# Q rows: two masked copies out of PSUM on VectorE, or one copy and two masks on GpSimd

## The chip, the cores and the metric

The kernel runs on one core of a Trainium2 chip. The metric is the device time of one execution, in microseconds (us); the time of a kernel is the median of several runs. A core has a matrix engine (PE, TensorE), which writes to PSUM; a vector engine (DVE, VectorE); an activation engine (ACT, ScalarE); GpSimd (POOL); and queues that start DMA transfers, most of them here on SyncE (SP). Each engine works through its own list of instructions in order and waits at semaphores for the others.

## The reference

Two identical transformer layers over one sequence of 2048 rows of 512 values, with 32 heads of 16 and a feed-forward width of 1792, all inputs in bf16:

```python
def _A_ref(x, wqkv, wo):                     # B, S, D = 1, 2048, 512; H = 32; Dh = 16
    qkv = (x @ wqkv).reshape(B, S, 3, H, Dh).transpose(2, 0, 3, 1, 4)
    q, k, v = qkv[0], qkv[1], qkv[2]
    scores = jnp.einsum("bhqd,bhkd->bhqk", q, k) * (Dh ** -0.5)
    p = _softmax(scores, axis=-1)
    o = jnp.einsum("bhqk,bhkd->bhqd", p, v)
    return o.transpose(0, 2, 1, 3).reshape(B, S, D) @ wo

def _B_ref(x, w_gate, w_up, w_down):         # F = 1792, gelu by tanh
    return (_gelu(x @ w_gate) * (x @ w_up)) @ w_down

x = x + _A_ref(_layernorm(x), A_wqkv, A_wo)
x = x + _B_ref(_layernorm(x), B_w_gate, B_w_up, B_w_down)
# ... and both once more, with the same weights
```

## The kernel before

**Units and tiles.** Attention is cut into units: one block of 512 queries (four per layer) and one group of four heads (eight per block), so 32 units per layer. A unit has 64 score tiles of 128 keys x 512 queries, 16 key tiles for each of its four heads. In the last block of the second layer a tile holds two key tiles of 256 queries instead, so that this block ends in two halves. Keys lie on the rows of a tile, queries on its columns.

**Scores and Q.** A head has only 16 rows of Q and K. PE is used in four row groups of 32, and each holds two heads, so one chunk of 128 rows holds eight heads: those of two units. To score one of the two heads of a row group, the rows of the other one must be zero in Q. So Q of a chunk is kept twice: copy 0 holds rows 0 to 15 of each 32 and zeros below, copy 1 the other way round. The function `qproj` builds the piece of work that projects Q: four matrix products into one PSUM bank (`mm_piece`, line 664), then two VectorE instructions (line 712) that read the bank and write the two copies as f16 into two of the six slots of `Q`. Each multiplies by a column of `QMASK`, [128, 2], which holds the scale `QSCALE` on the rows to keep and zero on the others. `QSCALE` carries the softmax scale and log2(e) x 1024, so that a score is a power of two in units of 1/1024. When both copies are there, `kept` announces the Q; the first twelve units' copies of the second layer are stored to DRAM (line 288, SP's queue) and read back later.

**Exp, on two engines.** Score products (line 1565) fill slots of three or two PSUM banks in turn, which ACT turns into exps with one instruction (line 1579, into `PT`). A further tile can go to a vector bank: DVE adds a bias, clips at zero and writes int16 (line 1619, into `PI`). Read as f16, these bits are a piecewise linear power of two. For its error three more copies are made, with the exponent shifted by one, two and three quarters of an octave (line 1659, into `PP`, SBUF to SBUF, up to four tiles in one instruction). All four are multiplied into V, the shifted ones into copies of V that are scaled down accordingly (`VD`, made by GpSimd, line 754). So a tile on ACT takes one product with V (called PV, line 1711), and a tile on DVE four. PV products of the four heads stand side by side in four column groups of PE and add up in bank 7; an extra column of ones in V gives the sum of exps. The sum of a unit is copied out (lines 1006 and 1011), sent through DRAM, divided by its sums of exps on GpSimd (line 967) and multiplied by `wo`.

**Other work.** Projections of K, Q and V, output products, and the feed-forward blocks (lines 1233 and 1297, evacuated by DVE at lines 1252, 1276 and 1328) are pieces that PE fits in between. Banks 5 and 6, when free, serve these pieces and the vector tiles. When PE has nothing to do, `keep_clock` adds a product with zeros into bank 7 (line 1731).

**The planner.** The order on every engine is decided before the program is built, by a Python loop that simulates all engines with fixed costs: an instruction of DVE or GpSimd has its cost as the last entry of its job. `vector_tile` allows a vector tile only if DVE's backlog (waiting jobs, and 0.48 us for each waiting shift) is below `DVE_LATE`. `fill_ready` says when the next slot may be filled; it may wait for a vector bank as long as ACT stays `WAIT_D` ahead. `pick` chooses the tiles of a slot, `flush` closes a group of shifts. `port_at` keeps the shifts of DVE and the work of GpSimd apart in the plan. `fit` is how many PV passes go before the next fill, and `post_tol` how far a feed-forward piece may run past it. `PACE` and `behind` set how fast each block's feed-forward is worked off while the next block's attention runs. On the chip each engine keeps the planned order, whatever the true durations are.

Of the kernel before, what the change touches and what calls it, by code (L numbers as in the profile page):

```python
# [175 lines left out]
def _emit_fast(nc, es, x_in, wqkv, wo, wg, wu, wd, out, n_rep=2):  # L176
# [21 lines left out]
    VW = 17  # L198
    NPH = 4
    NPART = 12 if NQB > 1 else 0  # L200
    DVE_LATE = 2.61
    WAIT_D = 0.65
    OCT = 1024.0
    LOG2E = 1.4426950408889634
    QSCALE = OCT * LOG2E * DH ** -0.5
# [31 lines left out]
    NQS = 6  # L237
# [36 lines left out]
    def bank(b):  # L274
        return PS[:, b, :]
# [34 lines left out]
    def change(kind):  # L310
        return SW if kind_now[0] != kind else 0.0
# [68 lines left out]

    sch.op("pool", lambda e: e.memset(QMASK[:], 0.0), w=[("QMASK",)])  # L381
    for j in range(4):
        sch.op("pool", lambda e, j=j: e.memset(QMASK[32 * j:32 * j + 16, 0:1], QSCALE), r=[("QMASK",)], w=[("QMASK",)])
    sch.op("pool", lambda e: e.tensor_scalar(QMASK[:, 1:2], QMASK[:, 0:1], -1.0, QSCALE, op0=ALU.mult, op1=ALU.add),
           r=[("QMASK",)], w=[("QMASK",)])
    sch.op("dve", lambda e: e.memset(PS[:, ACC, :], 0.0), w=[BK[ACC]], cost=0.6)
    sch.op("pool", lambda e: e.memset(OKV[:], 1.0), w=[("OKV",)])
# [281 lines left out]
    def xk(b):  # L669
        return [("XNT", 4 * b + i) for i in range(4)]  # L670
# [29 lines left out]
    def qproj(layer, up):  # L700

        qb, c = min(up // NCK, NQB - 1), up % NCK
        h = up // NCK - (NQB - 1) if layer == n_rep - 1 and NQB > 1 and up // NCK >= NQB - 1 else None
        q0, qn = (0, 512) if h is None else (256 * h, 256)

        qi = up + (NPART // 2 if layer and 2 * up >= NPART else 0)

        def evac(b):
            ops = []
            for p in range(2):  # L710
                slot = (layer * NU + 2 * qi + p) % NQS
                ops.append((lambda e, p=p, slot=slot: e.tensor_scalar(Q[:, slot, q0:q0 + qn], bank(b)[:, 0:qn],  # L712
                                                                     QMASK[:, p:p + 1], None, op0=ALU.mult),
                            [BK[b], ("QMASK",)], [("Q", slot)], 0.126 + 0.001042 * qn))
            evac_job(1, b, ops, kept)

        def kept(o):
            have.add((layer, "q", qi))
            if layer and 2 * up < NPART:
                for p in range(2):  # L720
                    u = 2 * up + p
                    slot = (layer * NU + u) % NQS
                    move(2, "qs%d" % slot, QSD[u, :, :], Q[:, slot, :], [("Q", slot)], [("QS", u)], got(("qs", u)), kb=128)
        lo = 512 * qb + q0
        return mm_piece([(WQ[:, ck, 128 * c:128 * (c + 1)], XNT[:, ck, lo:lo + qn]) for ck in range(NCK)],
                        [("XNT", t) for t in range(lo // 128, (lo + qn) // 128)] + [("WQ", c)], evac, cols=qn)
# [9 lines left out]
    def vproj(layer, c, kb):  # L736
        def fn(e, bs):
            for t in range(4):
                for ck in range(NCK):
                    tt = 4 * kb + t  # L740
                    ins = e.matmul(bank(bs[0])[:, 128 * t:128 * (t + 1)], lhsT=XNT[:, ck, tt * 128:(tt + 1) * 128],  # L741
                                   rhs=WV[:, ck, 128 * c:128 * (c + 1)], start=(ck == 0), stop=(ck == NCK - 1))
            return ins

        def then(o):
            have.add((layer, "v", c, kb))
            for part, (m0, m1) in (("A", (0, NMA)), ("B", (NMA, NM))):
                if m1 == m0 or kb != (3 * m1 - 1) // 4:
                    continue
                for ph in range(1, NPH):  # L750
                    dst = VD[:, c, ph - 1, :, 4 * m0:4 * m1, :]
                    src = AP(VP, (2 * c * NKT * 4 + 12 * m0 + 2) * VW,
                             [[VP[:].ap[0][0], 128], [NKT * 4 * VW, 2], [3 * VW, 4 * (m1 - m0)], [1, VW]])
                    job("pool", 2, [(lambda e, dst=dst, src=src, ph=ph: e.tensor_scalar(  # L754
                        dst, src, 2.0 ** (-ph / NPH), None, op0=ALU.mult),
                        [("VP", c, k) for k in range(kb + 1)] + [("VPONE",)], [("VD", c, part)],
                        0.46 + 0.039 * 4 * (m1 - m0))],
                        got((layer, "vd", c, part)) if ph == NPH - 1 else None)

        def after(bs):  # L760
            b = bs[0]
            evac_job(1, b, [(lambda e: e.tensor_copy(  # L762
                VP[:, c, :, 16 * kb:16 * kb + 16, 0:16].rearrange("p r k d -> p k r d"),
                bank(b).rearrange("p (k r d) -> p k r d", r=2, d=16)),
                             [BK[b]], [("VP", c, kb)], 0.6)], then)

        return Piece(0.064 * 4 * NCK, xk(kb) + [("WV", c)], fn, after)


    PRE = 1  # L770
# [645 lines left out]
    def vector_tile():  # L1416

        if pace["haste"]:
            return False
        if not dg["items"] and pend.get(("PI", dg["n"] % NPI)):  # L1420
            return False
        late = max(0.0, sch.free["dve"] - now[0]) + sum(op[3] for j in jobs["dve"] for op in j[2])
        late += 0.48 * len(shifts)
        return late < DVE_LATE

    def vector_bank():
# [11 lines left out]
    def pick(look=False):  # L1438

        cap = slot_cap()  # L1440
        want_d = not look and started_all() and behind() < LAG and vector_tile()
        bd = vector_bank() if want_d else None
        if bd is None or sch.ready("pe", w=[BK[bd]]) > now[0] + 0.13:
            want_d = False
        a, d = [], None
        spare = None
        for k, x in enumerate(cur):
            if len(a) == cap and (d is not None or not want_d or k >= 16):
                break
            t = x[3]  # L1450
            if want_d and d is None and d_tile(x) and (not dg["items"] or dg["uk"] == x[:3]):
                if all(y[3] % 4 != t % 4 for y in a):
                    d = x
                    continue
                if len(a) == cap and spare is None:
                    spare = x
            if len(a) < cap:
                a.append(x)
            elif not want_d:
                break  # L1460
        return a, d if d is not None else spare
# [17 lines left out]
    def fill_ready():  # L1479

        s = slot_no[0] % 2
        if slot_open[s]:
            return None
        if slot_no[0] < 2 and not free_banks.issuperset(slot_banks()):
            return None
        pull()
        a, _ = pick(True)
        a = [x for x in a if k_here(x)]
        if not a:
            return None  # L1490
        if pend.get(("PT", pt_of())):
            return None
        keys = []
        for x in a:
            keys += tile_keys(x)
        ready = sch.ready("pe", keys, [BK[b] for b in slot_banks()[:len(a)]])
        if started_all() and not pace["haste"] and (free_banks or vb_busy):
            free = min([sch.ready("pe", w=[BK[b]]) for b in free_banks]
                       + [max(sch.free["dve"], now[0]) + 0.78 for b in vb_busy])
            if ready < free <= sch.free["act"] - WAIT_D:  # L1500
                ready = free
        return ready
# [43 lines left out]
    def a_slot(atiles, dtile):  # L1546
# [50 lines left out]
        if dtile is not None:  # L1597
# [13 lines left out]
            def then(o):  # L1611
# [6 lines left out]
                ripe(items, gi, done)  # L1618
            dve(0, [(lambda e: e.tensor_scalar(PI[:, gi, 512 * r:512 * (r + 1)], bank(bd), DBIAS, 0.0,  # L1619
                                               op0=ALU.add, op1=ALU.max), [BK[bd]], [("PI", gi, r)], 0.6)], then)  # L1620
        if dg["items"] and (len(dg["items"]) == 4 or seg_left[dg["uk"]] < 4 and not any(
                x[:3] == dg["uk"] and d_tile(x) for x in cur)):
            flush()

# [168 lines left out]
    def post_source():  # L1793
        while True:
            if posts:
# [3 lines left out]
                for p in posts.pop(0):  # L1799
                    if p is not None:  # L1800
                        first += 1
                        if first <= 6:
                            p.tol = 1.0
                        pace["n"] += (p.cost + 0.1) / 0.71
                    yield p
# [9 lines left out]

    A_END = NU + NPART * (NQB - 1.0) / NQB
    B_END = A_END + NPART / NQB * min(1.0, NG / max(1.0, NPART))
    LAST = 2 * NU - NG / 2 + 2.00
    STEP = (LAST - B_END - 1.0) / (NQB - 1)
    PACE = [(NU + 1.0, A_END - 1.22)]  # L1820
    for i in range(NQB - 1):
        a = max(PACE[-1][1] if i else B_END + 1.0, NU + NG * (i + 1) + 1.0 if NG * (i + 1) > NPART else B_END + 1.0)
        PACE.append((a, LAST if i == NQB - 2 else B_END + 1.0 + STEP * (i + 1)))
# [16 lines left out]
    def post_tol():  # L1840
        if pace["haste"] or behind() > LAG:
            return 99.0
        return 0.45 if behind() > 0 else 0.17

    def queue_source(queue):
        while True:
# [14 lines left out]
    while True:  # L1861
# [27 lines left out]
            limit = max(F, sch.free["act"] - 0.44) - t  # L1889
        its = pv_ready(t)  # L1890
        byj = [sum(1 for it in its if it[1] == j) for j in range(4)]
        fit = int((limit - change("col")) / MM + 0.3)
        full = min(byj)
        rest = False
        if its:
# [8 lines left out]
        keep = next((p for p in (src.peek() for src in sources) if p is not None and p.held is not None), None)  # L1904
        ready_ = keep is not None and piece_ready(keep, keep.held) <= t + 0.02 and keep.cost + change("full") <= limit + 0.1
        if not (ready_ and not press) and fit >= 1 and (full >= want or full and (rest or press)):
            pv(its, min(fit, full, 4))
            continue
        cand = None
        for src in sources:  # L1910
# [883 lines left out]
```

## Time and profile before

| | |
|---|---|
| median of 4 runs | 1593.15 us (1591.34 to 1594.07) |
| profiled execution | 1591.3 us |
| its span, first to last instruction | 1589.0 us |
| granted TensorE clock | 1.0 |
| busy: PE, DVE, ACT, POOL | 1517.0, 1431.3, 1518.5, 177.8 us |

Busy time is the time in which an engine executes an instruction of the program. A row of the groups of instructions reads: line, engine, operation, what it writes <- what it reads, shapes, count, then the busy time in us and the mean length of one in ns, then the idle time of the engine just before these instructions and what ended it. Instructions of ACT overlap their neighbours a little, so their mean times their count is more than their busy time. A line of the timeline gives the start and the length of a run of equal instructions. A line of the table by stretches gives the stretch, its length, and the busy time (and number of instructions) of PE, PEld (its weight loads), DVE, ACT and POOL.

### The profile page before, as it was taken

The page shows a single profiled execution, that of the slowest core. Times are in us where ns is not written, and L with a number is a line of the kernel's source. Part 1 is how long each engine was busy: PE and PEld are TensorE (multiplying, and loading weights), DVE is VectorE, ACT ScalarE, POOL GpSimd, SP SyncE. Part 2 cuts the span into 40 slices and gives each one's busy share as a digit, 9 for nine tenths or more (in the row PEclk, how much of TensorE's full clock was granted, in tenths as well). Part 3 has the DMA queues.
Part 4 walks back from the last instruction along what each step waited for, and adds up shares of the span by engine and source line. Part 5 has one row for each costly group of instructions (what it writes and reads, how often), then busy time and mean ns, then how long its engine had stood idle before and what let it go on. Part 6 is the DMA issues. An engine that isn't in the chain of part 4 may idle for free.

```text
span 1589.0 us, 38476 instructions
## 1 busy us (share of the span) xinstructions
PE 1517.0 (95%) x16150; PEld 504.7 (32%) x16150; DVE 1431.3 (90%) x2485; ACT 1518.5 (96%) x1308; POOL 177.8 (11%) x218
## 2 busy tenths in 40 slices
PE   8999999999999999999999999899999999999998
PEld 4332222222222222333333223222222222444455
DVE  8999999889988899988998989999889889998784
ACT  6999999999999999999999999999999999999981
POOL 2311110011100211000520001020101000100010
PEclk9999999999999999999999999999999999999999
DMA  5200111125121411122512242332332114112145
GB/s 157 61 8 5 50 35 46 55 60 114 32 61 51 124 53 28 51 55 74 119 48 67 62 107 67 98 98 78 105 83 63 48 44 129 37 48 81 51 106 170
DMA packets 168377, 112.39 MB, mean 71 GB/s; under 512 B 55048, under 2 KB 148232, under 8 KB 168200
## 3 DMA queue, kind: packets, MB, share of 16 engines
q1 hardware_dynamic: 164504, 105.28, 24.6%
q0 software_dynamic: 2112, 4.19, 1.0%
q8 instruction: 131, 2.15, 0.6%
q10 hardware_dynamic: 1584, 0.39, 0.1%
q14 instruction: 46, 0.38, 0.1%
HBM read 81.40 MB, written 19.78 MB: 64 GB/s over the span
## 4 chain that ended last, share of the span: by engine, by line
ACT 44%; PE 44%; DVE 10%; DMA 1%; issue 1%; SPq 0%; DVEq 0%
ACT fPT L1579 41%; PE fPS L1711 13%; PE fPS L1565 12%; PE fPS L1233 10%; PE fPS L1297 5%; DVE fPI L1619 4%; DVE fPP L1659 4%; PE fPS L664 2%; ACT fHT L1525 2%; PE fPS L1731 1%; PE fPS L741 1%; ACT L1525 1%; DVE fHT L1252 0%; DVE fHT L1276 0%; ACT L1579 0%
## 5 line engine op out<-in xcount | busy, mean ns | idle before, releaser
L1579 ACT ACTIVATE fPT<-fPS 128x1536 bf16<-128x1536 f32 x1265 | 1444.5, 1281 | 23.7 <-PE fPS L1565 19.7
L1619 DVE TENSOR_SCALAR fPI<-fPS 128x512 int16<-128x512 f32 x935 | 632.9, 684 | 58.8 <-PE fPS L1565 53.4
L1565 PE MATMUL fPS<-fQ,fKT 32*128 32x512 f16 (+1 forms) x4608 | 504.0, 359 | 46.2 <-ACT fPT L1579 33.6
L1659 DVE TENSOR_SCALAR fPP<-fPI 128x2048 int16<-128x2048 int16 (+3 forms) x783 | 490.8, 646 | 12.3 <-PE fPS L1711 9.0
L1711 PE MATMUL fPS<-fPT,fVP 128*17 128x512 bf16 (+1 forms) x3555 | 452.9, 358 | 4.2 <-DVE fOS L1006 1.6
L1711 PE MATMUL fPS<-fPP,fVD 128*17 128x512 f16 (+1 forms) x3159 | 441.3, 357 | 4.5 <-DVE fPP L1659 3.7
L1565 PEld LDWEIGHTS fPS<-fQ,fKT 32*128 32x128 f16 x4608 | 135.3, 91 | 524.3 <-ACT fPT L1579 394.0
L1711 PE MATMUL fPS<-fPI,fVP 128*17 128x512 f16 (+1 forms) x1053 | 267.8, 358 | 1.4 <-DVE fOS L1006 0.7
L1233 PE MATMUL fPS<-fXNT,fWR 128*128 128x512 f16 (+1 forms) x952 | 219.6, 362 | 5.7 <-DVE fHT L1276 3.0
L1711 PEld LDWEIGHTS fPS<-fPT,fVP 128*17 128x17 f16 x3555 | 117.1, 88 | 144.1 <-issue 93.0
L1711 PEld LDWEIGHTS fPS<-fPP,fVD 128*17 128x17 f16 x3159 | 120.4, 89 | 113.0 <-issue 47.5
L967 POOL TENSOR_TENSOR fAT<-fOP,fRB 128x512 f16<-128x512 f32 (+1 forms) x35 | 43.5, 1243 | 692.2 <-DMA fRB<-rscr 640.9
L1297 PE MATMUL fPS<-fWR,fHT 128*128 128x512 bf16 x428 | 118.5, 383 | 0.6 <-DMA fWR<-in_B_w_down_dram 0.4
L1233 PEld LDWEIGHTS fPS<-fXNT,fWR 128*128 128x128 bf16 x952 | 77.1, 98 | 108.8 <-DVE fPI L1619 20.6
L1731 PE MATMUL fPS<-fONB,fZV 128*17 128x512 f16 x1292 | 105.3, 389 | 1.5 <-POOL fQMASK L381 1.5
L1276 DVE TENSOR_TENSOR fHT<-fPS,fHT 128x512 bf16<-128x512 f32 x112 | 76.5, 689 | 32.6 <-PE fPS L1233 22.3
L1711 PEld LDWEIGHTS fPS<-fPI,fVP 128*17 128x17 f16 x1053 | 69.4, 88 | 38.3 <-issue 16.4
L1252 DVE CAST fHT<-fPS 128x512 bf16<-128x512 f32 x105 | 72.1, 687 | 9.5 <-PE fPS L1233 8.8
L754 POOL TENSOR_SCALAR fVD<-fVP 128x544 f16<-128x544 f16 (+1 forms) x48 | 56.4, 1175 | 129.0 <-DVE fVP L762 126.4
L616 POOL TENSOR_SCALAR fLNS<-fMV 128x2 f32<-128x2 f32 (+1 forms) x28 | 8.2, 293 | 514.1 <-DVE fMV L607 513.8
L1525 ACT ACTIVATE fHT<-fHT 128x3584 bf16<-128x3584 bf16 (+1 forms) x16 | 47.3, 2997 | 7.3 <-DVE fHT L1252 7.2
L712 DVE TENSOR_SCALAR fQ<-fPS,fQMASK 128x512 f16<-128x512 f32 (+1 forms) x72 | 46.3, 685 | 3.9 <-PE fPS L664 3.9
(89 smaller groups left out, 626.2 us busy)
## 6 DMA issues: line engine op xcount, KB each, us to landing
fWR<-in_B_w_up_dram SPq DMA_DIRECT2D x62, 256.0 KB, 2.9
fWR<-in_B_w_down_dram SPq DMA_DIRECT2D x58, 256.0 KB, 2.8
fWR<-in_B_w_gate_dram SPq DMA_DIRECT2D x57, 256.0 KB, 4.2
oscr<-fOS SPq DMA_DIRECT2D x224, 32.0 KB, 1.7
fOP<-oscr SPq DMA_DIRECT2D x28, 256.0 KB, 2.8
fRB<-rscr SPq DMA_DIRECT2D x28, 256.0 KB
fX<-in_A_x_dram POOLq DMA_DIRECT2D x4, 1024.0 KB, 5.7
xscr<-fX SPq DMA_DIRECT2D x16, 256.0 KB, 2.1
```

The source lines that it names most:

```text
L754: job("pool", 2, [(lambda e, dst=dst, src=src, ph=ph: e.tensor_scalar(dst, src, 2.0 ** (-ph / NPH), None, op0=ALU.mult), [("VP", c, k) for ...
L1233: ins = e.matmul(bank(bs[0])[:, w * qn:(w + 1) * qn], lhsT=wchunk(s, (ft + w) % 2, ck), rhs=XNT[:, ck, xs], start=(ck == 0), stop=(ck == N ...
L1252: evac_job(1, b, [(lambda e: e.tensor_copy(in_ht(ft), in_bank(b)), [BK[b]], fk, 0.6)], got(("gate", layer, qb, h, ft)))
L1276: (lambda e: e.tensor_tensor(in_ht(ft), in_bank(b), in_ht(ft), op=ALU.mult), [BK[b]] + fk, fk, 0.62)], got(("up", layer, qb, h, ft))))
L1297: ins = e.matmul(bank(b)[:, 0:D], lhsT=HT[:, ft, i * 128:(i + 1) * 128], rhs=wslot(s)[:, jj * D:(jj + 1) * D], start=(ft == 0), stop=(ft = ...
L1525: sch.op("act", lambda e, lo=lo, hi=hi: e.activation(HT[:, lo:hi, q0:q0 + qn], HT[:, lo:hi, q0:q0 + qn], ACTF.Gelu_apprx_tanh), r=keys, w= ...
L1565: ins = e.matmul(bank(b)[:, b0:b0 + qn], lhsT=KT[32 * j:32 * j + 32, (x[1] % NG) // 2, kt * 128:(kt + 1) * 128], rhs=Q[32 * j:32 * j + 32, ...
L1579: o = sch.op("act", lambda e: e.activation(PT[:, at:at + na, :], PS[:, b0:b0 + na, :], ACTF.Exp, scale=1.0 / (OCT * LOG2E)), r=bks, w=[("P ...
L1619: dve(0, [(lambda e: e.tensor_scalar(PI[:, gi, 512 * r:512 * (r + 1)], bank(bd), DBIAS, 0.0, op0=ALU.add, op1=ALU.max), [BK[bd]], [("PI", ...
L1659: shifts.append((s, [(lambda e: e.tensor_scalar(PP[:, s, 0:512 * n], PI[:, gi, 0:512 * n], int(OCT) * ph // NPH, None, op0=ALU.add), [("PI ...
L1711: ins = e.matmul(PS[32 * j:32 * j + VW, ACC, 0:qn], lhsT=l, rhs=r_, start=a, stop=z, tile_position=(0, 32 * j), skip_group_check=True)
L1731: ins = e.matmul(PS[32 * j:32 * j + VW, ACC, :], lhsT=ZV[:, :], rhs=ones, start=False, stop=False, tile_position=(0, 32 * j), skip_group_c ...
```

## The change

One scaled copy of Q leaves PSUM on VectorE, into the slot of copy 0. From that slot GpSimd writes the masked copy 1 into the other slot, and then masks copy 0 in place. `kept` follows the second of these. The first Q of the first layer is still made by two VectorE copies. `QMASK` holds ones and zeros now, and `QSCALE` is an immediate number of the copy. Fourteen numbers of the planner get new values, all shown below.

```diff
-    DVE_LATE = 2.61
-    WAIT_D = 0.65
+    DVE_LATE = 2.82
+    WAIT_D = 0.45
...
-        sch.op("pool", lambda e, j=j: e.memset(QMASK[32 * j:32 * j + 16, 0:1], QSCALE), r=[("QMASK",)], w=[("QMASK",)])
-    sch.op("pool", lambda e: e.tensor_scalar(QMASK[:, 1:2], QMASK[:, 0:1], -1.0, QSCALE, op0=ALU.mult, op1=ALU.add),
+        sch.op("pool", lambda e, j=j: e.memset(QMASK[32 * j:32 * j + 16, 0:1], 1.0), r=[("QMASK",)], w=[("QMASK",)])
+    sch.op("pool", lambda e: e.tensor_scalar(QMASK[:, 1:2], QMASK[:, 0:1], -1.0, 1.0, op0=ALU.mult, op1=ALU.add),
...
+        slots = [(layer * NU + 2 * qi + p) % NQS for p in range(2)]
+
         def evac(b):
-            ops = []
-            for p in range(2):
-                slot = (layer * NU + 2 * qi + p) % NQS
-                ops.append((lambda e, p=p, slot=slot: e.tensor_scalar(Q[:, slot, q0:q0 + qn], bank(b)[:, 0:qn],
-                                                                     QMASK[:, p:p + 1], None, op0=ALU.mult),
-                            [BK[b], ("QMASK",)], [("Q", slot)], 0.126 + 0.001042 * qn))
-            evac_job(1, b, ops, kept)
+            if (layer, up) == (0, 0):
+                evac_job(1, b, [(lambda e, p=p: e.tensor_scalar(Q[:, slots[p], q0:q0 + qn], bank(b)[:, 0:qn],
+                                                                QMASK[:, p:p + 1], QSCALE, op0=ALU.mult, op1=ALU.mult),
+                                 [BK[b], ("QMASK",)], [("Q", slots[p])], 0.126 + 0.001042 * qn) for p in range(2)], kept)
+                return
+            evac_job(1, b, [(lambda e: e.tensor_scalar(Q[:, slots[0], q0:q0 + qn], bank(b)[:, 0:qn], QSCALE, None,
+                                                       op0=ALU.mult),
+                             [BK[b]], [("Q", slots[0])], 0.126 + 0.001042 * qn)], split)
+
+        def split(o):
+            job("pool", 0, [(lambda e, p=p: e.tensor_scalar(Q[:, slots[p], q0:q0 + qn], Q[:, slots[0], q0:q0 + qn],
+                                                            QMASK[:, p:p + 1], None, op0=ALU.mult),
+                             [("Q", slots[0]), ("QMASK",)], [("Q", slots[p])], 0.1 + 0.001 * qn) for p in (1, 0)], kept)
...
-        return Piece(0.064 * 4 * NCK, xk(kb) + [("WV", c)], fn, after)
+        return Piece(0.0557 * 4 * NCK, xk(kb) + [("WV", c)], fn, after)
...
-        late += 0.48 * len(shifts)
+        late += 0.6 * len(shifts)
...
-        if bd is None or sch.ready("pe", w=[BK[bd]]) > now[0] + 0.13:
+        if bd is None or sch.ready("pe", w=[BK[bd]]) > now[0] + 0.03:
...
-                       + [max(sch.free["dve"], now[0]) + 0.78 for b in vb_busy])
+                       + [max(sch.free["dve"], now[0]) + 0.69 for b in vb_busy])
...
-        if dg["items"] and (len(dg["items"]) == 4 or seg_left[dg["uk"]] < 4 and not any(
+        if dg["items"] and (len(dg["items"]) == 4 or seg_left[dg["uk"]] < 3 and not any(
...
-                        if first <= 6:
+                        if first <= 8:
...
-    LAST = 2 * NU - NG / 2 + 2.00
+    LAST = 2 * NU - NG / 2 + 2.14
...
-    PACE = [(NU + 1.0, A_END - 1.22)]
+    PACE = [(NU + 1.0, A_END - 0.76)]
...
-        return 0.45 if behind() > 0 else 0.17
+        return 0.40 if behind() > 0 else 0.1
...
-        fit = int((limit - change("col")) / MM + 0.3)
+        fit = int((limit - change("col")) / MM + 0.09)
...
-            pv(its, min(fit, full, 4))
+            pv(its, min(fit, full, 3))
```

## The prediction

> **What bounds the kernel now.** I read the page first (parts 1 and 2), then the groups of instructions by shape, the waits, and the engines' busy time in three stretches.
>
> ```profile
> PE 1517.0 (95%) x16150; PEld 504.7 (32%) x16150; DVE 1431.3 (90%) x2485; ACT 1518.5 (96%) x1308; POOL 177.8 (11%) x218
> ```
> ```profile
> 14.00:1520.00 1506.00, 1442.93 (x15279) 460.86 (x15279) 1377.69 (x2373) 1484.81 (x1274) 166.99 (x189) 1.00 0.25 66
> 1520.00:1589.00 69.00, 63.06 (x761) 38.96 (x753) 43.66 (x88) 31.16 (x32) 3.81 (x5) 1.00 0.48 137
> ```
> The second pair of lines gives the stretch, its length, then PE, weight loads, DVE, ACT and POOL. From 14 to 1520 us ACT is busy 1484.8 of 1506 us: it idles for 21 us in the whole body. PE idles 63 us there, but part of its busy time is padding. DVE idles 128 us. So three engines are near full, and ACT sets the pace. After 1520 us ACT's exps run out and PE works off what is left of the last feed-forward.
>
> ```profile
> L1579 ACT ACTIVATE fPT<-fPS 128x1536 bf16<-128x1536 f32 x1265 | 1444.5, 1281 | 23.7 <-PE fPS L1565 19.7
> L1619 DVE TENSOR_SCALAR fPI<-fPS 128x512 int16<-128x512 f32 x935 | 632.9, 684 | 58.8 <-PE fPS L1565 53.4
> L1659 DVE TENSOR_SCALAR fPP<-fPI 128x2048 int16<-128x2048 int16 (+3 forms) x783 | 490.8, 646 | 12.3 <-PE fPS L1711 9.0
> L1731 PE MATMUL fPS<-fONB,fZV 128*17 128x512 f16 x1292 | 105.3, 389 | 1.5 <-POOL fQMASK L381 1.5
> ```
> These four rows give the exchange rates. ACT does exps in 632 groups of three tiles, 632 of two and one single tile (the same group kept apart by shape): 3161 tiles in 1444.5 us, **0.457 us of ACT per tile**. DVE does the other 935, with 632.9 + 490.8 us: **1.20 us of DVE per tile**. Such a tile is multiplied into V four times instead of once. Four products stand side by side on PE for one pass of 0.216 us (the step from one full pass to the next), so three more are 0.16 us of PE. The last row is padding, zero products that keep PE's clock up: 1292 / 4 passes of 0.216 us are 70 us of PE that nothing waits for. A microsecond freed on DVE can therefore become ACT time only through the planner, as 1 / 1.20 tiles, worth 0.38 us.
>
> **What the change removes.**
> ```profile
> L712 DVE TENSOR_SCALAR fQ<-fPS,fQMASK 128x512 f16<-128x512 f32 x56 | 39.4, 745 | 3.7 <-PE fPS L664 3.7
> L1011 DVE COPY fOS<-fPS 128x512 f32<-128x512 f32 x56 | 38.3, 684 | 3.7 <-PE fPS L1711 2.8
> L712 DVE TENSOR_SCALAR fQ<-fPS,fQMASK 128x256 f16<-128x256 f32 x16 | 6.9, 476 | 0.2 <-PE fPS L664 0.2
> L1011 DVE COPY fOS<-fPS 128x256 f32<-128x256 f32 x16 | 6.7, 419 | 1.2 <-PE fPS L1711 1.0
> ```
> Q leaves PSUM 36 times, in two masked copies each: 28 of 512 columns (39.4 / 28 = 1.41 us a pair) and 8 of 256 (6.9 / 8 = 0.86). The first pair stays. In the other 35 one copy remains; its price is the row of another plain copy out of PSUM of that size, 0.684 and 0.419. DVE gains 27 x (1.41 - 0.684) + 8 x (0.86 - 0.419) = 19.6 + 3.5 = **23 us**, and a PSUM bank that pieces and vector tiles share comes free 0.7 us sooner 27 times.
>
> **What it adds on GpSimd.** 70 instructions. No row shows f16 from f16 without gaps; the nearest are these:
> ```profile
> L631 POOL TENSOR_SCALAR fHT<-fX,fLNS 128x512 f16<-128x512 f32 x36 | 33.4, 935 | 24.8 <-PE fPS L1297 23.1 <-PE fPS L1565 0.2
> L754 POOL TENSOR_SCALAR fVD<-fVP 128x544 f16<-128x544 f16 x24 | 41.1, 1714 | 83.3 <-DVE fVP L762 82.0
> ```
> I take the first (same width, no strided runs), 0.94 us, and half for 256: 54 x 0.94 + 16 x 0.47 = 58 us of an engine that is idle for 89% of the span. By the second it would be 54 x 1.71 + 16 x 0.86 = 106 us, still hidden. The POOL line's median of 774 ns gives 48 us as a low end. Behind them on POOL's queue stand the layernorm rows (L616 to L631), the attention's normalisation (L967), the scaled V copies (L754) and four loads of X; each may start one pair (1.9 us, at most 3.4) later. The normalisation waits 640.9 us for its DMAs, so its queue has room.
>
> Who waits for Q? I counted this from the times of the L712 pairs and of the score products, with 64 products a unit: apart from the first pair, a Q is ready 9.5 us (units 4 and 5 of the first layer) to 101 us before its first product. Two GpSimd copies of 1.9 us fit into the shortest lead, so this costs nothing; without that lead a late Q would stop PE and ACT by its own lateness. The twelve stores of the second layer's first Q rows wait for GpSimd instead of DVE in SP's queue, with weight loads behind them. They were issued from 671 us on and read back from 913 us: no cost for Q, and at most 6 x 1.9 = 11 us of delay for SP's loads, taken as zero as weights are loaded in seven slots ahead.
>
> **What GpSimd costs DVE.** This is the only real price:
> ```profile
> 403.00 2.37 DVE L1659 TENSOR_SCALAR fPP<-fPI 128x2048 int16<-128x2048 int16 x2
> 403.15 1.66 POOL L967 TENSOR_TENSOR fAT<-fOP,fRB 128x512 f16<-128x512 f32 x1 [24.44 <-DMA fRB<-rscr]
> ```
> Two shifts that take 0.68 us each alone took 2.37 us beside one POOL instruction: a shift and GpSimd exclude each other. Over the trace I compared the 2048-wide shifts that overlap a POOL instruction over 0.4 us (71, mean 852 ns) with the others (538, mean 685 ns): 71 x 0.167 = 12 us lost, beside 133 us of large POOL work (L754, L967, L631), or 0.09 us per us. For 58 us that is 5 us; ends 0 (a shift is never due then) and 54 x 0.94 + 16 x 0.47 = 58 us (each copy stops DVE for all its length). I take 5, as it is measured on the same two engines. Net on DVE: 23 - 5 = 18 us, 15 tiles, **15 x 0.457 = 6.9 us of ACT**. Their 15 x 0.16 = 2.4 us of PE come out of the 70 us of padding; in the feed-forward stretches, where there is almost none, they would cost time.
>
> In the Trainium skill, "SBUF — State Buffer", section "SBUF: two separate sides", the pair of ports that these engines share is an exclusive lock, held for the whole instruction, which speaks against the change. With that rule alone and shifts taking 34% of DVE's time, a copy of 0.94 us would stop DVE for about 0.3 us on average, some 20 us over 70 copies, and the gain would be 1 us instead of 7.
>
> **The settings.** They decide how many tiles DVE gets and how PE's gaps are filled. The allowed DVE backlog grows by 0.21 us, while each waiting shift counts 0.12 more: nearly even at two waiting shifts. A fill may wait for a vector bank until 0.45 us before ACT runs dry (0.65 before): more vector tiles, less cushion. V projections are priced at 0.0557 x 16 = 0.89 us; the trace has 56 ns between their products, 0.90 us for 16. Smaller tolerances for pieces and PV passes keep score products punctual and hold feed-forward pieces back. Nothing in the trace prices these together. Ends: ACT's whole 21 us of idle in the body gained, or as much again lost; the middle, zero, is nearest to the many small changes in both directions.
>
> **Sum.** The profiled execution took 1591.3 us (span 1589.0); 1591.3 - 6.9 = 1584.4. The median of the runs is 1.85 us higher, so against it 1593.15 - 6.9, rounded: **1586 us**.
>
> **The rivals.**
> - *Larger gain.* The freed bank and the new settings raise DVE's load by another 1% (15 us, 12 tiles, 5.7 us of ACT), and ACT's waits for score products, 19.7 us, shrink by a third: 1586 - 5.7 - 6.5 = 1574. For it: 128 us of idle DVE. Against: in stretches like 1080 to 1200 us PE is busy 118.3 of 120 us with hardly any padding, so more vector tiles there make PE late.
> - *Nothing gained.* The gap on DVE stays idle, since the feed-forward stretches are bound by PE and ACT together: 1593.
> - *Slower: PE is held back to the end.* Pieces refused by the smaller tolerances (0.10 for 0.17, 0.40 for 0.45) leave padding in the body and reappear after the last exp, where only PE works: 69 us now. Pieces are about 410 us of PE (1380 feed-forward products of L1233 and L1297 and 392 of L664 at 0.216 us, 512 V products at 0.056); if 5% slip, 20 us come back at the end: 1586 + 20 = 1606. It decides from 1.7% on (6.9 us). For it: after 1520 us PE is on the chain of the end. Against: the pacing is moved too.
> - *Slower: GpSimd stops DVE.* Place: the 35 splits. If each copy stopped a shift for its full length, DVE would lose 58 - 23 = 35 us net, 29 tiles, 13 us of ACT: 1606. It decides above 23 / 70 = 0.33 us a copy; measured was 0.09 per us.
> - *The change does not do what it says*: the planner may put the copies where DVE idles; that is the case without gain.
>
> **How the numbers follow.** Forecast 0.40, larger gain 0.16, nothing gained 0.10, held back 0.20, GpSimd 0.14. Two measurements of this kernel can be told apart from about 0.2%, 3.2 us: faster below 1590.0, slower above 1596.3. Faster gets 0.40 + 0.16 and a little of nothing gained: 0.58; slower 0.33, as one case in a hundred of GpSimd's stays within; same 0.09. The range runs from 1574 to 1606, leaving about 2 in 10 outside; the likeliest case alone spans 1580 to 1592 (contention of 0 or of 10 us gives 8.8 or 5.0 us of gain; the settings, a fifth of ACT's 21 idle us, 4 us either way).
>
> **What would show it.** Right: L712's successor has 35 fewer instructions and DVE 0.68 us each; POOL gains 70 of 0.6 to 1 us; L1619 rises from 935 to about 950, and L1579's tiles fall by as many; shifts' mean stays near 646 ns. Wrong: shifts' mean above 680 ns, vector tiles not more than 935, ACT idle in the body above 30 us, or a stretch after the last exp longer than 48 us (it starts at 1541.1 now).

## The result, and the profile after

The changed kernel takes 1591.85 us (median of 36 runs), against 1593.36 us (median of 59) before: a ratio of **0.9991**, with an interval of 0.9986 to 0.9996. That is a gain of about 1.4 us where 7 were forecast, and below the 0.2% from which the prediction tells two kernels apart. The profiled execution took 1590.2 us, its span is 1588.4.

The page of the changed kernel, busy times and the groups that answer to those shown of before (all lines behind `qproj` are eight higher than before):

```profile
PE 1510.4 (95%) x16116; PEld 502.6 (32%) x16116; DVE 1440.0 (91%) x2477; ACT 1513.2 (95%) x1298; POOL 293.5 (18%) x288
...
L1587 ACT ACTIVATE fPT<-fPS 128x1536 bf16<-128x1536 f32 x1255 | 1439.3, 1266 | 30.6 <-PE fPS L1573 25.6
L1627 DVE TENSOR_SCALAR fPI<-fPS 128x512 int16<-128x512 f32 x959 | 647.4, 684 | 54.7 <-PE fPS L1573 49.8
L1667 DVE TENSOR_SCALAR fPP<-fPI 128x2048 int16<-128x2048 int16 (+3 forms) x786 | 508.8, 666 | 11.9 <-PE fPS L1719 8.8
L1739 PE MATMUL fPS<-fONB,fZV 128*17 128x512 f16 x1168 | 97.9, 387 | 1.5 <-POOL fQMASK L381 1.5
```

The groups by shape, Q on both engines (GpSimd's masks are L721, VectorE's copies L716, the first pair L712):

```profile
L721 POOL TENSOR_SCALAR fQ<-fQ,fQMASK 128x512 f16<-128x512 f16 x54 | 94.5, 1750 | 564.9 <-DVE fQ L716 562.3
L721 POOL TENSOR_SCALAR fQ<-fQ,fQMASK 128x256 f16<-128x256 f16 x16 | 17.4, 1088 | 157.0 <-DVE fQ L716 156.2
L716 DVE TENSOR_SCALAR fQ<-fPS 128x512 f16<-128x512 f32 x27 | 18.5, 686 | 3.7 <-PE fPS L664 3.3
L716 DVE TENSOR_SCALAR fQ<-fPS 128x256 f16<-128x256 f32 x8 | 3.3, 415 | 0.0
L712 DVE TENSOR_SCALAR fQ<-fPS,fQMASK 128x512 f16<-128x512 f32 x2 | 1.4, 742 | 0.0
```

And the body by stretch (columns as before):

```profile
14.00:1520.00 1506.00, 1437.82 (x15238) 458.68 (x15235) 1385.89 (x2363) 1478.06 (x1263) 282.93 (x259) 1.00 0.25 66
```

What the reader sees: Q cost DVE 46.3 us before and costs 18.5 + 3.3 + 1.4 = 23.2 now. DVE turned that into **24 more vector tiles** (959 for 935), and ACT has ten groups fewer: five of three tiles, four of two and the single tile. But ACT idles 27.9 us in the body instead of 21.2, and a mask on GpSimd takes 1.75 us where the plan has 0.61. The shifts are 20 ns longer in the mean; half of that is mix, as fewer of them are narrow (at what each width takes alone, the mean rises from 629 to 640 ns).

Two measures, worked out from the trace's instructions, serve in all that follows. **Slack**: for each two neighbouring exps the step from start to start, less the median step of its width (1.331 us behind a group of three tiles, 0.905 behind two), summed. Left out are the long steps in which ACT works on the feed-forward (`fHT`, line 1525 of before): seven of 9 us each, 63 us in all, and an eighth of 6 us in `n1_wait` and `t2_wait65`. **Excess**: the time of the shifts above what each takes alone (685, 552, 418 and 283 ns for 2048 to 512 columns), summed over those that took longer. Slack rose from 50.0 to 62.6 us, excess from 14.2 to 22.5. A second profile of the same changed kernel (`after_again`) has 62.0 and 20.6, so slack is good to about 1 us and excess to about 2. The sum closes: up to the last exp's start there are five groups of each width less, 5 x (1.331 + 0.905) = 11.2 us of exps, the slack took 12.6 back, and the last exp starts at 1542.4 us instead of 1541.1; what follows it is 1.9 us shorter (46.0 for 47.9 us), and the span 0.5.

### The profile page after: what moved, and what is told of

The parts are those of the page before. It is cut to its first block, busy times and chain, and to the rows that moved or that the text cites. A ratio compares the mean times of both kernels' runs of the same rounds, so it can differ in the third digit from the quotient of the medians.

```text
span 1588.4 us, 38454 instructions
## 1 busy us (share of the span) xinstructions
PE 1510.4 (95%) x16116; PEld 502.6 (32%) x16116; DVE 1440.0 (91%) x2477; ACT 1513.2 (95%) x1298; POOL 293.5 (18%) x288
## 4 chain that ended last, share of the span: by engine, by line
ACT 41%; PE 40%; DVE 16%; issue 1%; POOL 1%; DMA 1%; SPq 0%; DVEq 0%
ACT fPT L1587 39%; PE fPS L1719 12%; PE fPS L1573 11%; PE fPS L1241 8%; DVE fPI L1627 6%; DVE fPP L1667 6%; PE fPS L1305 4%; PE fPS L664 3%; ACT fHT L1533 2%; PE fPS L1739 1%; PE fPS L749 1%; DVE fOS L1019 1%; DVE fHT L1260 1%; DVE fHT L1284 1%; ACT L1533 0%
## 5 line engine op out<-in xcount | busy, mean ns | idle before, releaser
L1627 DVE TENSOR_SCALAR fPI<-fPS 128x512 int16<-128x512 f32 x959 | 647.4, 684 | 54.7 <-PE fPS L1573 49.8
L1667 DVE TENSOR_SCALAR fPP<-fPI 128x2048 int16<-128x2048 int16 (+3 forms) x786 | 508.8, 666 | 11.9 <-PE fPS L1719 8.8
L1719 PE MATMUL fPS<-fPP,fVD 128*17 128x512 f16 (+1 forms) x3249 | 449.7, 357 | 5.1 <-DVE fPP L1667 3.6
L1719 PE MATMUL fPS<-fPI,fVP 128*17 128x512 f16 (+1 forms) x1083 | 271.1, 357 | 3.1 <-DVE fOS L1014 1.2
L721 POOL TENSOR_SCALAR fQ<-fQ,fQMASK 128x512 f16<-128x512 f16 (+1 forms) x70 | 111.9, 1599 | 721.9 <-DVE fQ L716 718.6
L1739 PE MATMUL fPS<-fONB,fZV 128*17 128x512 f16 x1168 | 97.9, 387 | 1.5 <-POOL fQMASK L381 1.5
L1019 DVE COPY fOS<-fPS 128x512 f32<-128x512 f32 (+1 forms) x72 | 45.0, 625 | 4.7 <-PE fPS L1719 3.1
```

The source lines that it names most:

```text
L721: job("pool", 0, [(lambda e, p=p: e.tensor_scalar(Q[:, slots[p], q0:q0 + qn], Q[:, slots[0], q0:q0 + qn], QMASK[:, p:p + 1], None, op0=ALU ...
L1667: shifts.append((s, [(lambda e: e.tensor_scalar(PP[:, s, 0:512 * n], PI[:, gi, 0:512 * n], int(OCT) * ph // NPH, None, op0=ALU.add), [("PI ...
L1719: ins = e.matmul(PS[32 * j:32 * j + VW, ACC, 0:qn], lhsT=l, rhs=r_, start=a, stop=z, tile_position=(0, 32 * j), skip_group_check=True)
L1739: ins = e.matmul(PS[32 * j:32 * j + VW, ACC, :], lhsT=ZV[:, :], rhs=ones, start=False, stop=False, tile_position=(0, 32 * j), skip_group_c ...
```

## The experiments

All ratios are against the kernel before, run beside them on the same chip. "Masks" says what GpSimd does for Q.

| kernel | settings | masks | ratio (interval) | vector tiles | slack us | excess us |
|---|---|---|---|---|---|---|
| before | old | none | 1 | 935 | 50.0 | 14.2 |
| changed | new | 1.75 us | 0.9991 (0.9986 to 0.9996) | 959 | 62.6 | 22.5 |
| e1_settings | new | none | 1.0016 (1.0007 to 1.0024) | 944 | 59.4 | 13.2 |
| e2_qonly | old | 1.75 us | 1.0029 (1.0018 to 1.0040) | 946 | 62.1 | 21.1 |
| e3_tiny | new | 2 columns | 0.9959 (0.9947 to 0.9972) | 959 | 59.5 | 16.7 |
| h1_qonly_tiny | old | 2 columns | 0.9983 (0.9973 to 0.9993) | 946 | 54.7 | 12.5 |
| e4_double | new | twice | 1.0124 (1.0109 to 1.0139) | 949 | 79.1 | 29.2 |
| k1_twoop | new | two operations | 0.9962 (0.9948 to 0.9975) | 959 | 59.5 | 18.0 |
| k4_twoop_vd | new | two operations, V copies too | 0.9944 (0.9930 to 0.9957) | 959 | 57.8 | 17.4 |

**The two halves of the change.** `e1_settings` is the kernel before with the new numbers; `e2_qonly` is the changed kernel with the old ones:

```diff
-    DVE_LATE = 2.82
-    WAIT_D = 0.45
+    DVE_LATE = 2.61
+    WAIT_D = 0.65
... and so on for all fourteen
```

> The kernel before with the fourteen numbers of the change alone; Q still leaves PSUM in two VectorE copies. Theory A (the gain of the Q copies is real and GpSimd takes it back, 1.6 us a mask and 8 us more of shifts held up): the settings are about neutral, 1591 to 1595 us, and the slack between ACT's exps (50 us before, 63 after) stays near 50. Theory B (the Q copies gain their 7 us and the new settings lose them, by a smaller cushion in front of ACT): slower, 1597 to 1602, slack about 60.

> The Q change with the old settings. Theory A: 1590 to 1594, POOL about 290 us busy, shifts about 20 ns longer in the mean than the 646 of before, slack above 55 us. Theory B: 1584 to 1588, slack near 50 us, about 945 vector tiles.

Each half alone is slower: 1596.28 and 1597.23 us, beside 1593.98 for before. `e1_settings` has 9 more vector tiles and none of GpSimd's masks, yet its slack is 59.4 us. So the new settings bring slack by themselves, as theory B has it, though less time than it claimed. (One plan stands for each setting here; how much a plan alone can do is looked at below.) `e2_qonly` is slower than either theory allowed, with an excess of 21.1 us. Neither theory holds alone.

**GpSimd's time, taken away and doubled.** Masks on 2 columns keep the plan and its planned costs; the Q rows are then not masked. The edit is shown in part: Q is also cleared once at the start, and halved:

```diff
-            job("pool", 0, [(lambda e, p=p: e.tensor_scalar(Q[:, slots[p], q0:q0 + qn], Q[:, slots[0], q0:q0 + qn],
+            job("pool", 0, [(lambda e, p=p: e.tensor_scalar(Q[:, slots[p], q0:q0 + 2], Q[:, slots[0], q0:q0 + 2],
```

> The changed kernel with its own plan, order and settings, but each GpSimd mask works on 2 columns instead of 512 or 256, so Q is not masked (the values of attention are left wrong; Q is halved so that its exps stay in range). It takes away the time that GpSimd holds, and nothing else. Theory A: the shifts' mean falls from 666 to about 645 ns, 8 to 10 us of DVE come back, slack falls to about 50 and the time to 1581 to 1586. Theory B: shifts as in A, but the time stays within 2 us of the changed kernel, 1590 to 1593.

> The Q change with the old settings, and masks on 2 columns (Q unmasked and halved, so attention's values are wrong): VectorE's saving without GpSimd's time. The prediction's own sum without contention, 8.8 us, gives 1584 to 1587 and slack near 50 us. If the old settings don't turn the freed time into vector tiles, 1590 to 1594 and slack near 60.

```profile
L722 POOL TENSOR_SCALAR fQ<-fQ,fQMASK 128x2 f16<-128x2 f16 x70 | 24.3, 348 | 754.2 <-DVE fQ L717 750.9
```

1586.87 us (0.9959), 0.32% or 5.1 us below the changed kernel, give or take 2; that lies between the two theories. The masks' busy time fell from 112 to 24 us, the excess by 5.8 us (3.9 against the second profile), the slack by 3.1. The shifts' mean is 659 ns and could not reach theory A's 645, as with this plan's widths it is 640 without any excess. With the old settings (`h1_qonly_tiny`, between its two expectations too) the same step is 1597.23 to 1590.32 us, 0.46% of before: its slack falls from 62.1 to 54.7. So in these two plans GpSimd's time costs 5 to 7 us. What is left of the slack is theory B's: 59.5 us with the new settings and no masks to speak of, nearly the 59.4 of `e1_settings`.

```diff
-                             [("Q", slots[0]), ("QMASK",)], [("Q", slots[p])], 0.1 + 0.001 * qn) for p in (1, 0)], kept)
+                             [("Q", slots[0]), ("QMASK",)], [("Q", slots[p])], (0.1 + 0.001 * qn) / 2) for p in (1, 1, 0, 0)], kept)
```

> The changed kernel with its own plan, and every GpSimd mask done twice (the second time over the same values), the planner charging the old price for both. POOL goes from 294 to about 400 us. Theory A: another 8 to 12 us of shifts held up and 1598 to 1605 us. Theory B: within 3 us of the changed kernel.

1612.78 us, more than either theory had. The planner's own order came out a little different (949 vector tiles), so it is no clean doubling. But its timeline shows a second way in which masks cost time:

```profile
796.97 3.65 POOL L721 TENSOR_SCALAR fQ<-fQ,fQMASK 128x512 f16<-128x512 f16 x2
...
800.59 1.56 POOL L762 TENSOR_SCALAR fVD<-fVP 128x544 f16<-128x544 f16 x1
802.13 1.26 POOL L975 TENSOR_TENSOR fAT<-fOP,fRB 128x512 f16<-128x512 f32 x1
...
803.53 1.87 PE L664 MATMUL fPS<-fWO,fAT 128*128 128x512 bf16 x4 [5.36 <-POOL fAT L975]
...
805.99 1.45 ACT L1587 ACTIVATE fPT<-fPS 128x1536 bf16<-128x1536 f32 x1 [6.59 <-PE fPS L1573]
```

Masks, a V copy and the normalisation stand in one queue. The normalisation comes late, PE waits 5.36 us for it in its own fixed order, and ACT 6.59 us for PE. The changed kernel has the same in small. These are GpSimd's instructions before 1062 us and PE's wait, and below them the same instructions of `k1_twoop` (see further down), which has this plan and shorter masks:

```profile
1042.94 3.35 POOL L721 TENSOR_SCALAR fQ<-fQ,fQMASK 128x512 f16<-128x512 f16 x2 [4.84 <-DVE fQ L716]
1046.27 1.70 POOL L975 TENSOR_TENSOR fAT<-fOP,fRB 128x512 f16<-128x512 f32 x1
1052.75 1.28 POOL L975 TENSOR_TENSOR fAT<-fOP,fRB 128x512 f16<-128x512 f32 x1 [4.78 <-DMA fRB<-rscr]
...
1060.58 1.27 POOL L975 TENSOR_TENSOR fAT<-fOP,fRB 128x512 f16<-128x512 f32 x1 [1.24 <-DMA fRB<-rscr]
...
1061.99 1.02 PE L664 MATMUL fPS<-fWO,fAT 128*128 128x512 bf16 x4 [0.56 <-POOL fAT L975]
```
```profile
1042.00 1.49 POOL L721 TENSOR_SCALAR fQ<-fQ,fQMASK 128x512 f16<-128x512 f16 x2 [5.46 <-DVE fQ L716]
1043.46 1.26 POOL L975 TENSOR_TENSOR fAT<-fOP,fRB 128x512 f16<-128x512 f32 x1
1049.55 1.28 POOL L975 TENSOR_TENSOR fAT<-fOP,fRB 128x512 f16<-128x512 f32 x1 [4.83 <-DMA fRB<-rscr]
...
1057.73 1.45 POOL L975 TENSOR_TENSOR fAT<-fOP,fRB 128x512 f16<-128x512 f32 x1 [1.71 <-DMA fRB<-rscr]
```

The masks start 0.9 us later in the changed kernel, the first normalisation 2.8 us, the next two 3.2 and 2.9 us, behind transfers that come later too (how the lateness passes through them was not traced). PE waits 0.56 us for the last one (0.78 in the second profile); with short masks that wait is gone.

A second wait, for a V copy at 785 us, is *not* the masks' doing. The changed kernel's lines stand first, those of `e1_settings`, which has no masks, below:

```profile
781.08 3.66 POOL L762 TENSOR_SCALAR fVD<-fVP 128x544 f16<-128x544 f16 x2
...
784.79 0.39 PE L1719 MATMUL fPS<-fPP,fVD 128*17 128x512 f16 x3 [0.66 <-POOL fVD L762]
...
786.20 1.02 ACT L1587 ACTIVATE fPT<-fPS 128x1024 bf16<-128x1024 f32 x1 [0.57 <-PE fPS L1573]
```
```profile
782.97 7.06 POOL L754 TENSOR_SCALAR fVD<-fVP 128x544 f16<-128x544 f16 x4
...
786.45 0.39 PE L1711 MATMUL fPS<-fPP,fVD 128*17 128x512 f16 x3 [0.66 <-POOL fVD L754]
```

It comes with the new settings' plan and V copies that follow each other; `e3_tiny` and `k1_twoop` have it too, the kernel before has no wait of PE for a V copy.

**How far a plan is a draw.** Changing one limit of the planner by 10 ns reorders much of the kernel:

```diff
-    WAIT_D = 0.65        (n1_wait; n2_late: DVE_LATE 2.61 to 2.62)
+    WAIT_D = 0.64
```

> The kernel before with WAIT_D 0.64 for 0.65, a change of 10 ns in one of the planner's limits, which redraws much of the order of work. Theory C (a plan is a draw, and the settings of each kernel were picked to hit a good one; that is why each half of the change alone is slower): 0.2 to 0.5% slower than before, 1596 to 1602 us, with slack between exps rising from 50 to 55 to 62 us. Theory D (the settings stand for real costs, and the halves are slower since the numbers fit one Q path and not the other): within 0.1% of before, 1592 to 1596, slack 48 to 53.

> The kernel before with DVE_LATE 2.62 for 2.61, another nudge of 10 ns. Theories C and D as for the kernel with WAIT_D 0.64: C 1596 to 1602 us with more slack, D 1592 to 1596.

> The changed kernel with WAIT_D 0.44 for 0.45. Theory C: slower than the changed kernel by 0.2 to 0.5%, 1594 to 1600 us. Theory D: within 0.1% of it, 1590.5 to 1594.

> The changed kernel with DVE_LATE 2.81 for 2.82. Theory C: 1594 to 1600 us. Theory D: 1590.5 to 1594. If the nudged pairs of both kernels keep the distance of 0.1%, that is the worth of the change apart from the draw.

The kernel before hardly minds: 0.9995 (0.9986 to 1.0004) and 0.9997 (0.9988 to 1.0006), slack 54 for both. The changed one does: 0.9975 (0.9966 to 0.9985) and 1.0044 (1.0031 to 1.0058), with 962 and 954 vector tiles, slack 61.2 and 66.5. Theory C fails for the one, theory D for the other; and C foresaw only losses, where one nudge made the changed kernel faster. Differences of some 0.3% between plans with the masks in them say nothing about a cause; the comparisons that count here keep the plan.

**The planned price, and one setting.** `t1_price` gives the masks their true cost in the plan, `t2_wait65` puts one setting back:

```diff
-                             ... [("Q", slots[p])], 0.1 + 0.001 * qn) for p in (1, 0)], kept)
+                             ... [("Q", slots[p])], 0.285 + 0.0025 * qn) for p in (1, 0)], kept)
```
```diff
-    WAIT_D = 0.45
+    WAIT_D = 0.65
```

> The changed kernel with the mask priced in the plan at 0.285 + 0.0025 x columns, what it takes (1.57 and 0.93 us), in place of 0.61 and 0.36. If the loss comes from a plan that puts other GpSimd work and shifts where the masks still run, the shifts' excess falls from 22 to about 15 us and the stalls at 785 and 1062 us go: 1587 to 1590. If GpSimd's time itself is the loss, wherever it lies, 1591 to 1596; a redrawn plan moves it by some 0.3% either way, so the excess and the waits on POOL count more here than the time.

> The changed kernel with WAIT_D back at 0.65. If the smaller cushion in front of ACT is what makes the slack between exps (63 us against 50), slack falls to 53 to 57 us and vector tiles fall from 959 to about 945; time 1589 to 1594. If the slack comes from elsewhere, it stays at 60 to 66.

`t1_price` is at 1.0009 (1.0000 to 1.0018). The excess fell to 15.0 us as expected, so the planner can keep shifts and masks apart once it knows their length. But PE now waits 1.2 us for a V copy at 781 us, and slack is 64.3: in this plan the lower excess bought no time. `t2_wait65` is at 1.0008 (0.9998 to 1.0018), slower than expected, with 931 vector tiles and a slack of 61.0 us: in the one plan tried, this setting alone is not what makes the slack. Both are other plans, so their times, within 0.2% of the changed kernel's, show no cause.

**Why a mask takes 1.6 us.** The nearest rows of before disagreed: 0.94 us for the layernorm row (f32 source), 1.71 for the V copies (f16, in runs of 17). `f1_f32` lets VectorE write f32 for GpSimd to read. `k1_twoop` changes the number of operations, since the layernorm row adds and multiplies and the V copy only multiplies:

```diff
-                                                            QMASK[:, p:p + 1], None, op0=ALU.mult),
+                                                            QMASK[:, p:p + 1], 0.0, op0=ALU.mult, op1=ALU.add),
```

> The changed kernel with the same plan, but VectorE's copy goes to an f32 buffer and GpSimd's two masks read that. In the trace of before GpSimd made f16 from 512 columns of f32 in 0.77 us; the masks from f16 took 1.57. If the source type is what doubles it, POOL's 112 us of masks fall to about 56, the shifts' excess falls by half of what the 2-column kernel saved, and the time lies halfway between the changed kernel and that one: 1588 to 1590.5 us. If not, it is the changed kernel's time, 1591 to 1593.

> The changed kernel, same plan, with a second operation in each mask: multiply by the mask, then add 0. If the number of operations is what doubles the mask's time, it falls from 1.57 to about 0.77 us, the 112 us of masks to about 57, the shifts' excess from 22 to about 19 us, and 0.6 of what the 2-column masks saved comes back: 1588 to 1589.5 us. If it is the multiplication or the source, 1591 to 1593 as before.

The f32 source changes nothing, 1.75 us again, ratio 1.0004 (0.9993 to 1.0015):

```profile
L722 POOL TENSOR_SCALAR fQ<-fQF,fQMASK 128x512 f16<-128x512 f32 x54 | 94.7, 1754 | 565.8 <-DVE fQF L717 563.2
```

The second operation does. The groups of `k1_twoop` and, below it, of `k4_twoop_vd`, in which the V copies get a second operation in the same way (a factor, then + 0.0):

```profile
L762 POOL TENSOR_SCALAR fVD<-fVP 128x544 f16<-128x544 f16 x24 | 41.4, 1727 | 70.3 <-DVE fVP L770 68.9
L721 POOL TENSOR_SCALAR fQ<-fQ,fQMASK 128x512 f16<-128x512 f16 x54 | 40.1, 742 | 586.1 <-DVE fQ L716 583.6
...
L721 POOL TENSOR_SCALAR fQ<-fQ,fQMASK 128x256 f16<-128x256 f16 x16 | 9.0, 562 | 158.8 <-DVE fQ L716 158.0
```
```profile
L721 POOL TENSOR_SCALAR fQ<-fQ,fQMASK 128x512 f16<-128x512 f16 x54 | 40.1, 743 | 593.6 <-DVE fQ L716 591.0
...
L762 POOL TENSOR_SCALAR fVD<-fVP 128x544 f16<-128x544 f16 x24 | 17.1, 714 | 74.6 <-DVE fVP L770 73.3
```

An instruction that does more takes 0.74 us in place of 1.75. In exactly the same plan the time falls to **1586.1 us**, 0.9962; the changed kernel, repeated on that chip, is at 0.9997 (0.9988 to 1.0006). That is 0.35%, all that the 2-column masks saved and more than the 0.6 of it that was expected.

> The changed kernel itself, once more, as the yardstick on this chip: 0.9986 to 1.0004 of before.

> As k1, and a second operation in GpSimd's scaled V copies too (1.57 us for 544 columns, 57 us in all). If the second operation halves them, another 25 us of GpSimd go and PE's wait for a V copy at 785 us with them: 1 to 2 us below k1. If these copies are slow because of their runs of 17, nothing changes against k1.

> The two-operation mask in the plan of the changed kernel with WAIT_D 0.44, which was the fastest so far at 0.9975 of before. If both gains add, 1586 to 1588 us, 0.9955 to 0.997 of before.

With the V copies treated alike (they fall from 1.73 to 0.71 us), `k4_twoop_vd` reaches **1585.12 us**, 0.9944 of before, and beats both kernels. PE's wait for a V copy at 785 us is gone. In the plan that was best with slow masks (WAIT_D 0.44) short masks bring 0.9975 to 0.9964 (0.9950 to 0.9977), a step within the noise. That is inside the range expected if both gains add, but that range was set before `k1_twoop` was seen; with its 0.35% the sum would be 0.994. So the masks' length costs 5 to 7 us in two plans and perhaps 2 us in a third.

> The kernel before, same plan, with a second operation (add 0) in GpSimd's scaled V copies. They fall from 56 to about 26 us. k4 gained 1 to 3 us from this over k1; here there are no masks in the queue, so at most that: 1590 to 1593 us, 0.998 to 1.0 of before.

> The Q change with the old settings, and two operations in masks and V copies. With masks of 1.57 us this was 1.0029 of before, with masks of 2 columns 0.9983. If the settings are what turns the freed time into vector tiles (959 with them, 946 without), it stays near 0.998 to 1.0, 1590 to 1593 us; if they don't matter, it reaches the 0.9944 of the same kernel with the new settings, 1584 to 1586.

The kernel before gains only 0.1% from faster V copies (0.999, 0.9981 to 0.9998); it had no wait of PE for them to lose. So with cheap GpSimd instructions on both sides the change comes to 0.9944 / 0.999 = 0.9954, some 7 us, give or take 2.5, for this pair of plans. With the old settings it is 0.998 (0.9970 to 0.9989) and 946 vector tiles: 0.36% of the time hang on the settings, or on the plan that they happen to give. One of the eleven runs of `m2_qonly_two` took 4030 us and is left out of its ratio; why it took so long is not known.

## Why the prediction was wrong

- *VectorE's saving: right.* 23 us were worked out, 46.3 - 23.2 = 23.1 measured, each copy at 0.686 and 0.415 us (0.684 and 0.419 taken).
- *GpSimd's masks: the step that failed.* I took the row that was nearest in shape, 0.94 us, and dismissed the slow row for its runs of 17. What set the duration was the number of operations. The masks took 112 us, 54 x 1.75 + 16 x 1.09, and not 58; even my upper end of 106 was below it. Of the signs named in advance this one told (masks of 0.6 to 1 us); none of the four signs of being wrong appeared. With the masks at 49 us and the plan unchanged (`k1_twoop`) 5.6 us come back.
- *What GpSimd costs DVE: right in kind, too small.* 5 us were taken, and the excess of the shifts rose by 8.3. The rate was not the error: 0.09 us per us on 112 us of masks would have been 10. (It set 12 us against 133 us of GpSimd's work, while its count took in every instruction over 0.4 us, 168 us in all: 0.07 us per us by one measure, and 0.06 in the changed kernel.) I had also charged this loss at 0.38 us per us of DVE, like a change of plan. In a fixed plan a late shift is not replanned: masks cut to 2 columns gave 5.1 us of time back for 5.8 us less excess and 0.6 us less waiting of PE for a normalisation. How the 5.1 us divide between the two is not shown.
- *POOL's queue: wrong in part.* "Its queue has room" held for Q itself: the trace shows nobody waiting for a mask. It did not hold where a normalisation is due behind masks: PE's 0.56 us at 1062 us, and 5.36 us with doubled masks. PE's wait for a V copy at 785 us comes without masks too.
- *The settings: not neutral, the second step that failed.* I put them at zero. Together with the Q change they give 24 more vector tiles (15 foreseen), 11.2 us of exps, where each alone gives 9 and 11. But the slack without masks to speak of is 59.5 us with them, against 50.0 before. Which of the fourteen does this, and how much of it is the draw of a plan, stays open; `WAIT_D` alone doesn't do it in the plan tried.
- *That `k1_twoop` meets the predicted 1586 us is in part luck.* Its masks take a little less than the prediction charged (49 us for 58), but it has 24 tiles less on ACT where 15 were foreseen, and some 9 us more slack where none was: two errors of the sum that work against each other. And the forecast gain, 0.4%, is of the size of what a nudge of 10 ns does to the changed kernel (0.16% faster, 0.53% slower).
- *PE's padding* gave way: 1168 / 4 passes of 0.216 us, 63 us for 70, where 2.4 us less were foreseen. The settings account for it rather than the vector tiles: `e1_settings` has 1164 such products at 944 tiles, `e2_qonly` 1252 at 946.
- *The rivals.* "GpSimd stops DVE" came nearest: its mechanism is there, at about a tenth of a us per mask in the shifts, below the 0.33 from which it would have made the kernel slower. "Nothing gained" has about the right time, by another way: DVE's freed time was used, and ACT's slack ate it, some 9 of the 12.6 us without the masks' part in it. PE was not held back to the end; the stretch after the last exp's start is shorter than before.

## What to carry to other kernels

Before work moves to an engine, look for a row of that engine with the same operation in the same form, not only the same shape and type; if two near rows differ twofold, keep both ends open, or measure the one instruction. Work that is "hidden" on an idle engine still shares a queue with things that others wait for, and where engines exclude each other its length has to be priced as well. In a kernel that is ordered ahead of time, compare causes in the same plan: two nudges of 10 ns left the changed kernel 0.7% apart.

## What the runs showed of the hardware

- GpSimd's `tensor_scalar` with one operation took 1.56 us on 512 columns when undisturbed, from f16 as from f32; with a second operation that adds zero it took 0.69 us (0.92 and 0.47 us on 256 columns). The V copies, whose factor is an immediate number, fell from 1.73 to 0.71 us in the mean in the same way. I had not expected that more work would be faster. The Trainium skill, in "GPSIMD Engine Reference", section "3.1 Elementwise — side-by-side cycle accounting", gives 768 ns for 512 elements as the best case of a tight loop: the form with two operations is near that (0.77 in the layernorm row, and 0.69 here, a little below it), and the masks and V copies with one take twice as long in every run here. Why is not shown.
- A shift of DVE and a GpSimd instruction held each other up in every kernel. In the changed one, 124 full-width shifts beside a GpSimd instruction of over 0.4 us took 831 ns in the mean, the other 503 took 684. It also shows in GpSimd's own time: 32 wide masks that met a shift took 1.88 us in the mean and 2.51 at most, the 22 that met none 1.57.
